# Weights' sign by a parametric ReLU, four q pairs shifted on VectorE, and the last attention product in 320 + 256 columns

## The chip, the cores and the metric

The kernel runs on one core of one Trainium2 chip. Its time is the device time of one launch in microseconds (us); lower is better. The kernel before took 1075.18 us, the median of 3 runs (1072.88 to 1076.26).

The engines are named as the profile names them. PE is TensorE, and PEld its weight loads. DVE is VectorE, ACT ScalarE (the engine of exp, ln and the other functions), POOL GpSimd. SP issues the transfers. Each engine runs its own instructions strictly in the order in which the program lists them; they wait for each other through semaphores.

## The reference

The work is a random-feature attention, and a two-layer network behind it:

```python
def phi(x):                                  # x is q or k, already scaled
    proj = np.einsum('bhsd,md->bhsm', x, omega)
    h = proj - np.sum(x * x, axis=-1, keepdims=True) / 2.0
    h = h - np.max(h, axis=-1, keepdims=True)
    return np.exp(h) / np.sqrt(m)
kv  = einsum('bhsm,bhsd->bhmd', phi(k), v);  z = sum_s phi(k)
out = einsum('bhsm,bhmd->bhsd', phi(q), kv) / (einsum('bhsm,bhm->bhs', phi(q), z) + 1e-6)
x = out.transpose(0, 2, 1, 3).reshape(4608, 512)
h = x @ w_in                                 # 512 -> 2048
g = h * erf(softplus(h))
return g @ w_out                             # 2048 -> 512
```

There are 8 batches, 8 heads, 576 tokens, 64 dimensions a head, and 128 random features. `w_in` and `w_out` arrive in float64; the kernel gets their bits as int64.

## The kernel before

**Attention.** Two heads make a pair, so there are 4 pairs a batch and 32 in all. A pair has 2 x 576 = 1152 token rows, in 9 chunks of 128. For k, and then for q, PE projects the chunks into three PSUM banks (`ppk`, `ppq`), DVE takes the negated maximum of each row (`mxk`, `mxq`), and ACT computes exp(projection + negated maximum), one instruction for each chunk, because the maximum is a bias with one value for each partition (`fk`, `fq`). PE multiplies `fk` with v (`kvp`), turns `fq` round by transposes (`pt`), and multiplies the two (`nd`), in spans of the 576 tokens: 384 columns, and then 192. ACT takes 1/denominator as exp(-ln(nd)) (`rc`), and DVE multiplies (`xs`). The first 8 pairs (batches 0 and 1) do this in plain float32; their squares (`uk`, `uq`) come from POOL or ACT and go into the projection. The other 24 pairs work with two-part numbers, a high part and a rest, in three matmuls each (`kh`/`kl`, `qh`/`ql`). There the squares are summed apart (`sk`, `sq`), and a pair of small DVE instructions (`shift`) puts them into the maxima.

**Network.** `h` (and `hX`, `hY`, `hZ` from the fourth batch on) is the first product, `o` the second; each is a sum of three matmuls of 288 columns, with weights in a high part and a rest. Between them stand softplus (`gs<-hs`), erf (`gs<-gs`), the gate, and the split of the result (`gh`, `gl`).

**Weights.** A unit of 128 x 512 weights comes as float64 bits (`st`) and is made into float32 in a PSUM tile (`wt`), 32 units in all, in the order in which the first batch needs them. Before the change a unit takes six steps: ACT scales the upper words by 2^-112 (`w_bias`, a Copy), DVE shifts left by 3 (`w_shift`), DVE puts the sign bit in (`w_sign`), DVE puts the last 3 bits in (`w_tail`), ACT rounds the high part (`w`), DVE takes the rest (`w`). A made unit is written back to DRAM (`wdw`) and fetched in later batches.

**The order.** `build` lists every operation with engines, costs and a due time, and `Plan.order` plays them through on a model of five engines, the ready operation with the earliest due time first. What comes out is the fixed order of each engine, and which of several engines takes a step (squares may go to POOL or ACT). `FIRST`, the time that a pair of the first batch is planned to take, sets the due times of the first batch, and by `START0` those of all that follow. The model charges ACT a change of function table only for operations that name a set (`set="exp"`, `"sp"`, `"erf"`), and holds other named sets back between the softplus and the erf of a chain (`lock`). The weights' steps name no set. Where the built program needs a table that isn't loaded, a load (ACT_TABLE_LOAD) is put in front of the instruction.

All compute instructions are recorded through one helper, so the profile gives them one line, L824; they are told apart by tile names. A name such as `uk_0_3` is batch 0, pair 3.

Of the kernel before, what the change touches and what calls it, by code (L numbers as in the profile page):

```python
# [19 lines left out]
P = 128  # L20
# [10 lines left out]
T = 288  # L31
# [273 lines left out]
SPANS = ((0, 384), (384, 192))  # L305

BLOCKS = ((("f", 0), ("f", 1)), (("e", 0),), (("f", 2),), (("e", 1),), (("f", 3),), (("e", 2),), (("e", 3),))
WHOLE = 8
PLAIN = 3
ROWS = 8  # L310
PAIR = 8.6
FIRST = 11.5
# [17 lines left out]
def build(emit):  # L330
# [46 lines left out]
    def make(u, t):  # L377
# [9 lines left out]
        pl.op("psign", [("V", 0.68, -1e9)], lambda e: E.w_sign(st, w), reads=[(st, 0), (w, 0)],  # L387
              writes=[(w, 0)])
# [109 lines left out]
    def project(n, qk, t0):  # L498
# [15 lines left out]
        else:  # L514
# [5 lines left out]
            order = range(3)  # L520
        for i in order:
            c = chunks[i]
            pl.op("max" + qk, [("V", 0.15 + 0.135 * len(c), -1e9)],
                  lambda e, i=i, c=c: E.maximum(mx, banks[i], c),
                  reads=[(banks[i], 0)], writes=[(mx, k) for k in c])
        if rows:
            sq = a["s" + qk]
            pl.op("less", [("V", 0.33, -1e9)], lambda e: E.shift(mx, sq),
                  reads=[(mx, k) for k in range(NC)] + [(sq, 0)], writes=[(mx, k) for k in range(NC)])
        for i in order:  # L530
            c = chunks[i]
# [275 lines left out]
def tile_attention_moe(ctx: ExitStack, tc: tile.TileContext, qT, kT, qR, kR, qN, kN, vP, omT, w1, w2, out):  # L807
# [68 lines left out]
    class Emit:  # L876
# [8 lines left out]
        def w_bias(self, e, t, w):  # L885
            dst, src = w.ap.bitcast(F32), t.ap[:, :, 1].bitcast(F32)
            if e == "A":
                act.activation(dst, src, AF.Copy, scale=2.0 ** -112)
            else:
                pool.tensor_scalar(dst, src, 2.0 ** -112, 0.0, op0=ALU.mult, op1=ALU.add)  # L890
# [275 lines left out]
```

## Time and profile before

| | before |
|---|---|
| median of 3 runs | 1075.18 us (1072.88 to 1076.26) |
| the profiled execution's own time | 1073.78 us |
| its span in the profile | 1072.0 us |
| granted TensorE clock, mean | 0.998 |
| PE busy | 1051.2 us, 8272 matmuls |
| DVE busy | 734.6 us |
| ACT busy | 719.4 us, 92 table loads among them |
| POOL busy | 352.1 us |

A row of the timeline gives start, length, engine, operation, out<-in, shapes and count, and in brackets the idle time before it with what ended that. A row of the windows gives a stretch, its length, and for each engine the busy time and instructions, then the granted clock, the share of time the DMA engines were busy, and GB/s. A row of the waits gives who waited for whom: the sum, how often, the longest. Matmuls are pipelined, so the distance from one start to the next tells what one costs, not its length.

### The profile page before, as it was taken

To read this page: it belongs to the slowest core of one execution; us is meant where nothing else is said; L and a number is where in the kernel's file an instruction comes from. 1 tells how busy PE (TensorE), PEld (TensorE's weight loads), DVE (VectorE), ACT (ScalarE), POOL (GpSimd) and SP (SyncE) were. 2 spreads that over 40 slices of the span, in tenths; PEclk is the share of its full clock that TensorE was granted. 3 is DMA by queue.
4 is the path that set the end of the run, shared out by engine and by line. 5 is a ranking of instruction groups with operands and counts; after the bars stand their busy time and mean duration, and the time that the engine had idled before them with its cause. 6 is when DMAs were issued, how large, how long until landed. Compare 5 with 4: busy or idle time off the path is not lost.

```text
span 1072.0 us, 21687 instructions
## 1 busy us (share of the span) xinstructions
PE 1051.2 (98%) x8272; PEld 1025.9 (96%) x8272; DVE 734.6 (69%) x1316; ACT 719.4 (67%) x1390; POOL 352.1 (33%) x306
## 2 busy tenths in 40 slices
PE   7899899999999999999999999999999999999998
PEld 7798899999999999999999999999999999999998
DVE  4889988877488586965768566766658656564431
ACT  7878878875668565867657666775667765564540
POOL 6222104100066294812334312522127222263330
PEclk9999999999999999999999999999999999999999
DMA  8376568776557777587776767768675775668771
GB/s 229 119 239 223 204 235 269 251 256 203 201 197 262 251 260 265 172 279 260 256 238 217 259 231 254 253 210 278 229 252 188 278 234 204 205 204 295 264 244 47
DMA packets 97382, 247.02 MB, mean 230 GB/s; under 512 B 10976, under 2 KB 11360, under 8 KB 97280
## 3 DMA queue, kind: packets, MB, share of 16 engines
q1 hardware_dynamic: 97216, 245.57, 67.9%
q8 instruction: 66, 1.08, 0.4%
q14 instruction: 36, 0.29, 0.1%
q0 software_dynamic: 64, 0.07, 0.0%
HBM read 210.99 MB, written 34.60 MB: 229 GB/s over the span
## 4 chain that ended last, share of the span: by engine, by line
PE 92%; DMA 3%; DVE 3%; ACT 1%; issue 1%; SPq 0%; POOL 0%; DVEq 0%; POOLq 0%; ACTq 0%
PE o L824 37%; PE h L824 13%; PE hX L824 12%; PE hY L824 6%; PE kvp L824 5%; PE nd L824 5%; PE ppq L824 4%; PE ppk L824 4%; PE hZ L824 3%; PE pt L824 2%; DMA st<-w 1%; DVE wt L824 1%; DMA uq<-qN 1%; DMA w<-wdw 1%; DVE xs L824 0%
## 5 line engine op out<-in xcount | busy, mean ns | idle before, releaser
L824 PE MATMUL o<-gh,w 128*128 128x288 f32 x2048 | 445.2, 298 | 0.2 <-ACT fq L824 0.2
L824 PEld LDWEIGHTS o<-gh,w 128*128 128x128 f32 x2048 | 339.3, 188 | 2.3 <-ACT fq L824 0.5
L824 PE MATMUL o<-gl,w 128*128 128x288 f32 x1024 | 301.7, 295 | 0.0
L824 PEld LDWEIGHTS o<-gl,w 128*128 128x128 f32 x1024 | 192.6, 188 | 0.0
L824 PE MATMUL h<-xh,w 128*128 128x288 f32 x768 | 174.6, 303 | 6.3 <-DVE w L824 2.8
L824 PE MATMUL hX<-xh,wb 128*128 128x288 f32 x640 | 162.0, 299 | 0.0
L824 PEld LDWEIGHTS h<-xh,w 128*128 128x128 f32 x768 | 129.7, 190 | 9.3 <-DVE w L824 4.5
L824 ACT ACT_TABLE_LOAD x92 | 118.0, 1283 | 2.3 <-PEq L1157 0.7
L824 PE MATMUL h<-xl,w 128*128 128x288 f32 x384 | 113.9, 297 | 0.0
L824 PEld LDWEIGHTS hX<-xh,wb 128*128 128x128 f32 x640 | 113.5, 188 | 0.4
L824 POOL TENSOR_TENSOR uk<-uk 128x288 f32<-128x288 f32 (+1 forms) x54 | 49.4, 934 | 181.4 <-DMA uk<-kN 119.9
L824 POOL TENSOR_TENSOR uq<-uq 128x288 f32<-128x288 f32 (+1 forms) x46 | 42.4, 942 | 184.5 <-DMA uq<-qN 66.1
L824 POOL TENSOR_TENSOR gl<-hs,gh 128x576 fp32r<-128x576 f32 x50 | 89.4, 1809 | 39.7 <-ACT gh L824 29.4
L824 PE MATMUL hX<-xl,wb 128*128 128x288 f32 x320 | 94.6, 296 | 0.0
L824 DVE TENSOR_REDUCE mxk<-ppk 128x4 f32<-128x512 f32 (+2 forms) x96 | 50.7, 553 | 62.1 <-PE ppk L824 61.1
L824 POOL TENSOR_TENSOR hs<-gs,hs 128x576 f32<-128x576 f32 x26 | 42.9, 1669 | 149.5 <-ACT gs L824 149.5
L824 DVE TENSOR_TENSOR hs<-gs,hs 128x1152 f32<-128x1152 f32 x51 | 81.2, 1600 | 13.4 <-ACT gs L824 13.4
L824 ACT ACTIVATE hs<-hX 128x288 f32<-128x288 f32 x75 | 30.8, 410 | 85.8 <-PE hX L824 82.9
L824 ACT ACTIVATE fq<-ppq,mxq 128x128 f32<-128x128 f32 x288 | 78.6, 386 | 13.5 <-DVE mxq L824 13.2
L824 ACT ACTIVATE rc<-nd,eps 64x192 f32<-64x192 f32 (+1 forms) x128 | 63.6, 497 | 33.3 <-PE nd L824 30.7
L824 ACT ACTIVATE fk<-ppk,mxk 128x128 f32<-128x128 f32 x288 | 79.9, 385 | 3.8 <-DVE mxk L824 3.3
L824 PE MATMUL hY<-xh,wb 128*128 128x288 f32 x320 | 81.3, 299 | 0.0
(106 smaller groups left out, 2115.9 us busy)
## 6 DMA issues: line engine op xcount, KB each, us to landing
w<-wdw SPq DMA_DIRECT2D x144, 512.0 KB, 4.9
wb<-wdcS SPq DMA_DIRECT2D x160, 256.0 KB, 4.1
wb<-wdw SPq DMA_DIRECT2D x120, 256.0 KB, 3.9
st<-w SPq DMA_DIRECT2D x32, 512.0 KB, 5.1
wdw<-w SPq DMA_DIRECT2D x32, 512.0 KB, 3.7
v<-vP SPq DMA_DIRECT2D x32, 325.0 KB, 4.3
out<-os SPq DMA_DIRECT2D x32, 288.0 KB, 3.6
wdcS<-cS SPq DMA_DIRECT2D x16, 512.0 KB, 5.1
```

What stands on the lines that cost most here:

```text
L824: return tc.keep_in_program_order(method(*args, **kwargs))
```

## The change

- **Sign.** `w_bias` becomes a parametric ReLU with scale 2^-112 and alpha -2^32. A negative word comes out positive, with its exponent 32 higher, and the shift by 3 moves that bit to the sign's place. `w_sign` goes, on all 32 units: three DVE steps instead of four.
- **q of the first four pairs.** For the pairs of batch 0, DVE adds the negated maximum to the projection, one instruction for each three chunks (`less`), and ACT takes one exponential over all nine chunks in place, instead of nine.
- **Raw maxima in PSUM.** In the 24 two-part pairs the maxima are written behind the middle chunk's bank in PSUM; the two small instructions read them there, the first writes back there, the second writes `mx`.
- **Spans.** `nd`, `rc` and `xs` work on 320 + 256 columns instead of 384 + 192, in all 32 pairs.
- **Planner.** `FIRST` goes from 11.5 to 10.0 (so `START0` from 51 to 45), and the cost of `nd` is written anew.

```diff
-SPANS = ((0, 384), (384, 192))
+SPANS = ((0, 320), (320, 256))
 WHOLE = 8
+LESS = [(n, "q") for n in range(NP)]
-FIRST = 11.5
+FIRST = 10.0
...
-        pl.op("psign", [("V", 0.68, -1e9)], lambda e: E.w_sign(st, w), reads=[(st, 0), (w, 0)],
-              writes=[(w, 0)])
...
+        less = (n, qk) in LESS
...
-                  lambda e, i=i, c=c: E.maximum(mx, banks[i], c),
-                  reads=[(banks[i], 0)], writes=[(mx, k) for k in c])
+                  lambda e, i=i, c=c: E.maximum(E.raw(banks[1]) if rows else mx.ap, banks[i], c),
+                  reads=[(banks[i], 0)], writes=[(banks[1], ("m", i))] if rows else [(mx, k) for k in c])
...
+            if less:
+                pl.op("less" + qk, [("V", 0.56, -1e9)], lambda e, i=i, c=c: E.less(f, mx, banks[i], c),
+                      reads=[(banks[i], 0)] + [(mx, k) for k in c], writes=[(f, k) for k in c])
+                continue
...
+        if less:
+            pl.op("exp" + qk, [("A", 1.16, -1e9)], lambda e: E.exponential_all(f),
+                  reads=[(f, k) for k in range(NC)], writes=[(f, k) for k in range(NC)], set="exp")
...
-                pl.op("nd", [("T", (4 if n < WHOLE else 3) * COST["mm"] * w / T, -1e9)],
+                pl.op("nd", [("T", w / 600 if n < WHOLE else 3 * max(0.111, 0.012 + w / 2400), -1e9)],
...
         def w_bias(self, e, t, w):
-                act.activation(dst, src, AF.Copy, scale=2.0 ** -112)
+            act.activation(w.ap.bitcast(F32), t.ap[:, :, 1].bitcast(F32), AF.Prelu, scale=2.0 ** -112,
+                           alpha=-2.0 ** 32)
...
-            for x in (-half_sq, half_sq):
-                dve.scalar_tensor_tensor(mx.ap, sq.ap, x, mx.ap, op0=ALU.mult, op1=ALU.add)
+            for dst, x in ((raw, -half_sq), (mx.ap, half_sq)):
+                dve.scalar_tensor_tensor(dst, sq.ap, x, raw, op0=ALU.mult, op1=ALU.add)
+
+        def less(self, f, mx, b, c):
+            n = len(c)
+            dve.tensor_add(f.ap[:, c[0]:c[0] + n, :], b.ap[:, :n * P].rearrange("p (c m) -> p c m", c=n),
+                           mx.ap[:, c[0]:c[0] + n].rearrange("p (c m) -> p c m", m=1).broadcast_to([P, n, P]))
+
+        def exponential_all(self, f):
+            act.activation(f.ap, f.ap, AF.Exp)
```

Since the planner decides the order, three places of the built program are shown. The first is DVE at q of batch 0, pair 1, and the first weight unit. Before:

```order
L824 TENSOR_REDUCE mxq_0_1_263<-ppq_0_1_0_253 128x3
L824 TENSOR_SCALAR wt1_0_0_257<-wt1_0_0_257 128x512
L824 TENSOR_REDUCE mxq_0_1_263<-ppq_0_1_1_259 128x3
L824 TENSOR_REDUCE mxq_0_1_263<-ppq_0_1_2_267 128x3
L824 SCALAR_TENSOR_TENSOR wt1_0_0_257<-st1_0_0_152,wt1_0_0_257 128x512 x2
L824 COPY kh_0_1_313<-kvp_0_1_287 128x2x64
```

And after:

```order
L832 TENSOR_REDUCE mxq_0_1_263<-ppq_0_1_0_250 128x3
L832 TENSOR_TENSOR fq_0_1_271<-ppq_0_1_0_250,mxq_0_1_263 128x384
L832 TENSOR_REDUCE mxq_0_1_263<-ppq_0_1_1_258 128x3
L832 TENSOR_REDUCE mxq_0_1_263<-ppq_0_1_2_267 128x3
L832 TENSOR_TENSOR fq_0_1_271<-ppq_0_1_1_258,mxq_0_1_263 128x384
L832 TENSOR_TENSOR fq_0_1_271<-ppq_0_1_2_267,mxq_0_1_263 128x384
L832 TENSOR_SCALAR wt1_0_0_254<-wt1_0_0_254 128x512
L832 COPY kh_0_1_302<-kvp_0_1_278 128x2x64
```

Three shifts came between the maxima, and of the unit's two steps on `st` (x2) one is left, which now stands further down.

The second place is ACT at the same pair, from the first unit's `wt` on. Before:

```order
L824 ACTIVATE wt1_0_0_257<-st1_0_0_152 128x512
L824 ACTIVATE rc_0_0_0_265<-nd_0_0_0_0_237,eps_68 64x384
L824 ACTIVATE rc_0_0_0_265<-nd_0_0_1_0_242,eps_68 64x384
L824 ACTIVATE fq_0_1_275<-ppq_0_1_0_253,mxq_0_1_263 128x128 x3
L824 ACTIVATE fq_0_1_275<-ppq_0_1_1_259,mxq_0_1_263 128x128 x3
L824 ACTIVATE fq_0_1_275<-ppq_0_1_2_267,mxq_0_1_263 128x128 x3
```

And after:

```order
L832 ACTIVATE wt1_0_0_254<-st1_0_0_154 128x512
L832 ACTIVATE rc_0_0_0_243<-rc_0_0_0_243 128x320
L832 ACTIVATE rc_0_0_1_265<-nd_0_0_0_1_245,eps_68 64x256
L832 ACTIVATE rc_0_0_1_265<-nd_0_0_1_1_247,eps_68 64x256
L832 ACTIVATE rc_0_0_1_265<-rc_0_0_1_265 128x256
L832 ACTIVATE uk_0_3_221<-uk_0_3_221 64x1152
L832 ACTIVATE wt1_0_1_292<-st1_0_1_160 128x512
L832 ACTIVATE fq_0_1_271<-fq_0_1_271 128x1152
```

The exponential of pair 1's q now stands behind the reciprocals of pair 0, the square of k of pair 3 (`uk_0_3`, POOL's work before) and a second unit's `wt`.

The third place is ACT at the second chain of softplus and erf (`gs` of the first batch, blocks 2 and 3). Before:

```order
L824 ACT_TABLE_LOAD
L824 ACTIVATE gs0_0_2_1190<-hs0_0_2_981 128x1152
L824 ACTIVATE w1_1_2_11_1030<-wt1_1_2_1109 128x2x256
L824 ACTIVATE w1_1_3_12_1053<-wt1_1_3_1118 128x2x256
L824 ACTIVATE gs0_0_3_1191<-hs0_0_3_1103 128x1152
L824 ACTIVATE wt2_0_0_0_1224<-st2_0_0_0_1194 128x512
L824 ACT_TABLE_LOAD
L824 ACTIVATE gs0_0_2_1190<-gs0_0_2_1190 128x1152
```

And after:

```order
L832 ACT_TABLE_LOAD
L832 ACTIVATE gs0_0_2_1097<-hs0_0_2_954 128x1152
L832 ACTIVATE w1_1_2_11_1000<-wt1_1_2_1054 128x2x256
L832 ACT_TABLE_LOAD
L832 ACTIVATE wt1_1_3_1141<-st1_1_3_1071 128x512
L832 ACTIVATE qh_1_1_1125<-pt_1_1_1_1137 128x384
L832 ACT_TABLE_LOAD
L832 ACTIVATE gs0_0_3_1098<-hs0_0_3_1047 128x1152
L832 ACT_TABLE_LOAD
L832 ACTIVATE wt2_0_0_0_1161<-st2_0_0_0_1100 128x512
L832 ACT_TABLE_LOAD
L832 ACTIVATE gs0_0_2_1097<-gs0_0_2_1097 128x1152
```

Each `wt` that falls between softplus and erf now has a table load of its own, and one brings softplus back where another softplus follows. The whole program has 102 table loads instead of 92: one more at the first chain, three more at each of the second, third and fifth.

More of the change, by code (lines that the diff above doesn't have):

```diff
@@ L523, in project @@
             pl.op("max" + qk, [("V", 0.15 + 0.135 * len(c), -1e9)],
-                  lambda e, i=i, c=c: E.maximum(mx, banks[i], c),
-                  reads=[(banks[i], 0)], writes=[(mx, k) for k in c])
+                  lambda e, i=i, c=c: E.maximum(E.raw(banks[1]) if rows else mx.ap, banks[i], c),
+                  reads=[(banks[i], 0)], writes=[(banks[1], ("m", i))] if rows else [(mx, k) for k in c])
         if rows:
             sq = a["s" + qk]
-            pl.op("less", [("V", 0.33, -1e9)], lambda e: E.shift(mx, sq),
-                  reads=[(mx, k) for k in range(NC)] + [(sq, 0)], writes=[(mx, k) for k in range(NC)])
+            keys = [(banks[1], ("m", i)) for i in order]
+            pl.op("less", [("V", 0.34, -1e9)], lambda e: E.shift(mx, E.raw(banks[1]), sq),
+                  reads=keys + [(sq, 0)], writes=keys[:1] + [(mx, k) for k in range(NC)])
         for i in order:
             c = chunks[i]
+            if less:
+                pl.op("less" + qk, [("V", 0.56, -1e9)], lambda e, i=i, c=c: E.less(f, mx, banks[i], c),
+                      reads=[(banks[i], 0)] + [(mx, k) for k in c], writes=[(f, k) for k in c])
+                continue
             pl.op("exp" + qk, [("A", 0.371 * len(c), -1e9)],
@@ L885, in w_bias @@
         def w_bias(self, e, t, w):
-            dst, src = w.ap.bitcast(F32), t.ap[:, :, 1].bitcast(F32)
-            if e == "A":
-                act.activation(dst, src, AF.Copy, scale=2.0 ** -112)
-            else:
-                pool.tensor_scalar(dst, src, 2.0 ** -112, 0.0, op0=ALU.mult, op1=ALU.add)
+            act.activation(w.ap.bitcast(F32), t.ap[:, :, 1].bitcast(F32), AF.Prelu, scale=2.0 ** -112,
+                           alpha=-2.0 ** 32)
         def w_shift(self, w):
             dve.tensor_scalar(w.ap, w.ap, 3, None, op0=ALU.logical_shift_left)
-        def w_sign(self, t, w):
-            dve.scalar_tensor_tensor(w.ap, t.ap[:, :, 1], -2 ** 31, w.ap,
-                                     op0=ALU.bitwise_and, op1=ALU.bitwise_or)
         def w_tail(self, t, w):
@@ L969, in project_mid, with raw, shift @@
             pe.matmul(b.ap[:, :P], lhsT=u.ap[:, NC * D + WIDE:], rhs=wr, start=True, stop=True)
+        def raw(self, mid):
+            return mid.ap[:, P:P + NC]
         def maximum(self, mx, b, c):
             n = len(c)
-            dve.tensor_reduce(mx.ap[:, c[0]:c[0] + n], b.ap[:, :n * P].rearrange("p (c m) -> p c m", c=n),
+            dve.tensor_reduce(mx[:, c[0]:c[0] + n], b.ap[:, :n * P].rearrange("p (c m) -> p c m", c=n),
                               axis=AX.X, op=ALU.max, negate=True)
-        def shift(self, mx, sq):
-            for x in (-half_sq, half_sq):
-                dve.scalar_tensor_tensor(mx.ap, sq.ap, x, mx.ap, op0=ALU.mult, op1=ALU.add)
+        def shift(self, mx, raw, sq):
+            for dst, x in ((raw, -half_sq), (mx.ap, half_sq)):
[6 more added lines that the diff above has]
+            act.activation(f.ap, f.ap, AF.Exp)
         def exponential(self, f, mx, b, c):
```

## The prediction

> **What bounds the kernel now.** I read the page's busy line first, then the windows, then who PE waited for.
>
> ```profile
> span 1072.0 us, 21687 instructions
> PE 1051.2 (98%) x8272; PEld 1025.9 (96%) x8272; DVE 734.6 (69%) x1316; ACT 719.4 (67%) x1390; POOL 352.1 (33%) x306
> ```
>
> PE is idle for 1072.0 - 1051.2 = 20.8 us in all. The windows say where:
>
> ```profile
> 0.00:52.00 52.00, 43.15 (x299) 38.06 (x300) 34.01 (x72) 42.16 (x120) 22.70 (x28) 1.00 0.65 179
> 52.00:100.00 48.00, 46.05 (x351) 44.45 (x349) 43.07 (x78) 39.12 (x82) 12.85 (x13) 1.00 0.67 225
> 100.00:150.00 50.00, 45.56 (x330) 42.38 (x330) 45.94 (x73) 40.48 (x79) 5.91 (x5) 0.97 0.56 194
> 150.00:200.00 50.00, 48.53 (x374) 46.52 (x374) 42.04 (x71) 40.63 (x84) 13.35 (x17) 1.00 0.78 271
> 200.00:1040.00 840.00, 839.72 (x6713) 826.60 (x6713) 562.97 (x1015) 555.47 (x1025) 293.15 (x242) 1.00 0.71 240
> 1040.00:1072.00 32.00, 28.15 (x213) 27.92 (x211) 6.57 (x10) 1.58 (x2) 4.13 (x3) 0.99 0.20 71
> ```
>
> From 200 to 1040 us PE idles for 0.3 us of 840: nothing done on DVE, ACT or POOL there can show, only PE's own work. The last 32 us lose 3.9 us, with hardly anything on ACT or DVE. What is left is the first 200 us: 8.9 us lost by 52 us (the first batch's attention), 2.0 + 4.4 from 52 to 150, 1.5 to 200. Whatever those 200 us gain or lose moves all that follows by as much, since what follows is PE alone. In 52 to 150 us DVE is the fuller helper, 43.07 + 45.94 = 89.0 of 98 us (91%), and ACT has 39.12 + 40.48 = 79.6 (81%).
>
> PE's waits up to 52 us:
>
> ```profile
> PE kvp L824 <- ACT fq L824: 1.3, 1, 1.3
> PE ppq L824 <- ACT fq L824: 0.9, 1, 0.9
> ```
>
> and from 52 to 210 us (sum, how often, longest):
>
> ```profile
> PE h L824 <- DVE w L824: 2.8, 3, 1.6
> PE h L824 <- ACT w L824: 1.6, 1, 1.6
> ```
>
> Early it is exponentials of q that hold a PSUM bank (1.3 + 0.9); later it is weight units not yet made (2.8 + 1.6).
>
> **The change part by part.** *Spans, in the 24 two-part pairs.* Starts of PE in one pair, columns in the shape:
>
> ```profile
> 227.03 0.29 PE L824 MATMUL h<-xl,w 128*128 128x288 f32 x1
> ...
> 227.29 0.34 PE L824 MATMUL nd<-qh,kh 128*128 128x384 f32 x1
> ...
> 227.81 0.25 PE L824 MATMUL nd<-qh,kh 128*128 128x192 f32 x1
> ...
> 228.46 0.32 PE L824 MATMUL h<-xh,w 128*128 128x288 f32 x1
> ```
>
> Two matmuls of 288 columns take 227.29 - 227.03 = 0.26, so 0.130 each; three of 384 take 0.52, so 0.173 each; six of 192 take 0.65, so 0.108 each. So 96 columns cost 0.043 above 288 and only 0.022 below it: 192 columns are too few to be worth their price. 320 lies a third of the way from 288 to 384, 0.144. 256 is 0.123 on the line from 192 to 288 and 0.116 on the line from 384 to 288 carried on. Against 0.173 + 0.108 = 0.281 the new pair of spans is 0.267 or 0.260, and there are 24 x 2 x 3 = 144 such couples: -2.1 or -3.1 us. If 256 cost as much as 288, -1.0. I take -2.5, and all of it counts, since it is PE's own work and most of it lies beyond 200 us. The eight float32 pairs have the same columns in all and a cost per column, so nothing there. ACT and DVE get the same 576 columns in two pieces as before.
>
> *Sign.* 64 DVE steps on `st` become 32:
>
> ```profile
> L824 DVE SCALAR_TENSOR_TENSOR wt<-st,wt x64: 681/695/730, 21.6 to 237.4; 128x512 int32<-128x512 int32 x64
> L824 ACT ACTIVATE wt<-st x32: 608/636/692, 19.3 to 233.8; 128x512 f32<-128x512 f32 x32
> ```
>
> That is 32 x 0.695 = 22.2 us off DVE, of which some 18 units, 12.5 us, lie between 52 and 150 us: DVE goes from 91% to 78% there. A parametric ReLU on ACT doesn't stand in this trace; the nearest row is the Copy it replaces (0.636), and the other functions of one immediate scale have the same rate by element, so I take 0.636, no change.
>
> *Table loads.* The order of the built program has ten more: one at the first chain of softplus and erf, three each at the second, third and fifth. The price of one, and what follows it:
>
> ```profile
> L824 ACT ACT_TABLE_LOAD x92 | 118.0, 1283 | 2.3 <-PEq L1157 0.7
> ...
> 96.39 0.88 ACT L824 ACTIVATE fk<-ppk,mxk 128x128 f32<-128x128 f32 x3
> 97.29 1.28 ACT L824 ACT_TABLE_LOAD   x1
> 98.58 1.16 ACT L824 ACTIVATE gs<-hs 128x1152 f32<-128x1152 f32 x1
> ```
>
> From the end of `fk` (97.27) to the start of softplus (98.58) is 1.31: a load costs its own 1.283. Seven of the ten fall before 150 us: 9.0 us, and ACT there goes from 79.6 to 88.6 of 98 us, 90%. So DVE and ACT change places. The three of the fifth chain lie beyond 200 us, where ACT is busy for 66% of the time, and are covered; uncovered they would be 3.8. The planner charges none of the ten. Behind the loads of the second chain stand the exponentials of k and q of batch 1's pair 2, and behind those, on PE, that pair's products. Bounds for 52 to 150 us: at best PE loses none of the weights' waits, -4.4, and with the clock that fell to 0.97 in 100 to 150 us (some 1.5 us of 50) -5.9; at worst the four loads of the first two chains come through to PE uncovered, 4 x 1.283 = +5.1 (the third chain's three then run while PE works off what it has). I take -1.0: ACT has 9.4 us left for the loads, so part of DVE's relief comes through.
>
> The Trainium skill, "ScalarE: Activation LUTs", section "What ACT_TABLE_LOAD costs", puts every change of set at about 1283 ns for the load and another 1380 ns of drain, some 2.66 us. By that the seven loads would be an estimated 18.6 us, more than ACT has left; the rows above show the 1283 and no drain behind it.
>
> *q of the first four pairs, and the start.* ACT's work for one q, the landing that matters, and the nearest row for the new steps of DVE:
>
> ```profile
> 17.81 0.93 ACT L824 ACTIVATE fk<-ppk,mxk 128x128 f32<-128x128 f32 x3
> 19.31 0.64 ACT L824 ACTIVATE wt<-st 128x512 f32<-128x512 f32 x1 [0.57 <-DMA st<-w]
> 19.98 1.18 ACT L824 ACTIVATE rc<-nd,eps 64x384 f32<-64x384 f32 x2
> 21.18 2.43 ACT L824 ACTIVATE fq<-ppq,mxq 128x128 f32<-128x128 f32 x9
> ...
> 25.93 2.25 POOL L824 TENSOR_TENSOR uk<-uk 64x576 f32<-64x576 f32 x2 [2.50 <-DMA uk<-kT]
> 26.24 1.07 PE L824 MATMUL pt<-ident,fq 128*128 128x128 f32 x6
> ...
> 52.45 0.43 PE L824 MATMUL h<-xh,w 128*128 128x288 f32 x1
> ...
> L824 DVE TENSOR_TENSOR ql<-pt,qh x72: 543/557/560, 188.7 to 920.5; 128x384 fp32r<-128x384 f32 x72
> ```
>
> One exponential over 1152 columns, 1.16 as the softplus above, for nine in 2.43: ACT saves 1.3 a pair, 5.1 in all. DVE pays three subtractions of 384 columns out of PSUM, 3 x 0.557 = 1.7 a pair, 6.7 in all, less 2.1 for the three signs that fall before 52 us: +4.6, on 34.0. The bank of `ppq` is freed by DVE now, so the 1.3 + 0.9 of PE's waits on `fq` should go.
>
> But ACT's order hides a new wait. The 25.93 row is the square of k of pair 3, which POOL could begin only when the tile had landed. The DMA engines are full until then:
>
> ```profile
> 20.00:26.00 6.00, 4.70 (x42) 4.50 (x41) 4.58 (x11) 5.83 (x17) 3.43 (x5) 1.00 1.03 290
> 26.00:30.00 4.00, 3.19 (x17) 1.76 (x16) 3.75 (x8) 3.56 (x12) 3.92 (x4) 1.00 0.26 96
> ```
>
> and SP's order puts the same bytes ahead of it as before (a weight unit moved up, but both units stood ahead already). So it lands at about 25.9 again, and the change puts this square on ACT, in front of `fq` of pair 1. ACT, done with `fk` at 18.74, has 3.6 us of `wt` and reciprocals (0.64 + 1.18, and about as much for the rest of pair 0) and reaches the square at 22.3; it stands until 25.9, then 1.16 (a square has the same 1152 columns), 0.64 and 1.16 bring `fq` of pair 1 at 28.9. Before, PE began that pair's transposes at 26.24. Queued behind are `fk` of pair 2 on ACT, and DVE's copies of `qh` behind PE's transposes. That is +2.7, with DVE's 4.6 closing some of the room to make it up, +1.0; less the 2.2 of waits that go: +1.5 by 52 us. Bounds: -2.2 (the square is made up for) and +3.7 (the waits on `fq` only change their name).
>
> *Raw maxima.* The two small instructions of each q and k of the 24 pairs are short, and begin late:
>
> ```profile
> L824 DVE SCALAR_TENSOR_TENSOR mxq<-sq,mxq x48: 170/171/1352, 167.7 to 907.9; 128x9 f32<-128x9 f32 x48
> ```
>
> Their number stays; only their operand moves. What 9 columns cost out of PSUM no row tells: not less than 0.170, and not more than the 0.557 above for 384 columns out of PSUM. Over 2 x 48 of them that is at most 96 x 0.387 = 37 us of DVE, which has 277 of 840 us free where most lie, and PE waits for no one there: 0 for the time, and nothing of the range. *FIRST* is only an order, and is in the places above.
>
> Sum: -2.5 - 1.0 + 1.5 = -2.0. The profiled execution took 1073.78 (span 1072.0 and 1.8 around it), so 1071.8; it stands 1.4 below the median, 1075.18, so for the median **1073.2 us**.
>
> **The rivals.** *Faster.* DVE's relief decides. For it: DVE is the fuller helper now, and three of PE's waits name its weights. Against: ACT takes on in the same stretch most of what DVE sheds. Waits on `fq` gone (-2.2), waits on weights gone (-4.4), spans -2.5: -9.1, 1066.
>
> *Slower.* ACT becomes the bound at the second chain. For it: seven loads in 98 us that the planner didn't count, in front of pair 2's exponentials, and an ACT already late from the start. Against: 9.4 us of ACT idle in that stretch. It decides as soon as ACT's busy share in 100 to 150 us goes above about 95%. Price: +2.7 from the start, +5.1 from four loads, -2.5: +5.3, 1080.5. One variant is that a load held ACT for longer than its own 1.28: with a drain as long again, four loads would cost 5.5 more, and the time would be 1086; the gap of 0.01 between load and softplus speaks against it, so 0.02 of the chance below. (That variant is the skill's rule named above.)
>
> *Near the forecast.* The two cancel, and PE's own 2.5 is what is left.
>
> **How the numbers follow.** About 0.3%, 3.2 us, is what a measurement of this kernel can tell from no change. Forecast 0.47, faster 0.33, slower 0.20. The forecast's own range is 1070 to 1077; of its chance 0.08 lies below 1072.0 and the rest is "same". Of the faster case 0.05 falls inside the 0.3%, of the slower 0.03, and 0.02 of the forecast's ends above. So faster 0.36, same 0.45, slower 0.19. All best bounds together give -3.1 - 5.9 - 2.2 = -11.2 (1064), all worst -1.0 + 5.1 + 3.7 = +7.8 (1083); the range, 1065 to 1079.5, leaves out about one in ten on each side.
>
> **What would show it.** Spans: starts of `nd` 0.144 and about 0.12 apart. Loads: 102 of 1.28 each, and ACT near 90% from 52 to 150 us. The start: ACT idle for 3 us or more before `uk`, named DMA, and the first `h` at 54 us or later instead of 52.45. The sign: no wait of PE for DVE's weights, and waits for ACT's `fk`, `fq` or `qh` in their place. Wrong would be: the first `h` before 51 us; PE losing less than 3 us between 52 and 150 (then 1066); more than 10 (then 1080); or any loss of several us beyond 200 us.

## The result: 0.6 to 0.8% slower

The changed kernel took 1084.06 us (median of 6 runs, 1079.27 to 1086.90), the kernel before 1075.09 in the same comparison: a ratio of 1.0083, with a 95% interval of 1.0056 to 1.0109. Timed twice more it took 1080.80 and 1081.02, ratios 1.0057 (1.0038 to 1.0075) and 1.0057 (1.0044 to 1.0071). The median of all 15 runs is 1081.37, and they spread over 7.6 us. Forecast were 1073.2, in a range of 1065 to 1079.5, and 1080.5 for the slower rival.

### The profile page after: what moved, and what is told of

It reads as the page before. It is cut to its first block, busy times and chain, and to the rows that moved or that the text cites. A ratio compares the mean times of both kernels' runs of the same rounds, so it can differ in the third digit from the quotient of the medians.

```text
span 1082.6 us, 21638 instructions
## 1 busy us (share of the span) xinstructions
PE 1052.5 (97%) x8272; PEld 1026.7 (95%) x8272; DVE 742.7 (69%) x1319; ACT 710.6 (66%) x1343; POOL 364.0 (34%) x319
## 4 chain that ended last, share of the span: by engine, by line
PE 87%; DVE 4%; ACT 4%; DMA 3%; issue 1%; POOL 1%; SPq 1%; DVEq 0%; ACTq 0%; POOLq 0%
PE o L832 35%; PE h L832 12%; PE hX L832 12%; PE hY L832 6%; PE kvp L832 5%; PE nd L832 4%; PE ppq L832 4%; PE ppk L832 3%; PE hZ L832 3%; PE pt L832 3%; ACT L832 1%; DMA uk<-kT 1%; ACT gs L832 1%; DVE wt L832 1%; DMA v<-vP 1%
## 5 line engine op out<-in xcount | busy, mean ns | idle before, releaser
L832 PE MATMUL h<-xh,w 128*128 128x288 f32 x768 | 177.0, 305 | 9.2 <-DVE hs L832 2.9
L832 ACT ACT_TABLE_LOAD x102 | 130.9, 1283 | 2.5 <-PEq L1169 0.7
L832 POOL TENSOR_TENSOR uk<-uk 128x288 f32<-128x288 f32 (+1 forms) x54 | 54.7, 1033 | 174.5 <-DMA uk<-kN 129.8
L832 ACT ACTIVATE rc<-nd,eps 64x256 f32<-64x256 f32 (+1 forms) x128 | 63.5, 496 | 44.8 <-PE nd L832 42.8
L832 DVE TENSOR_TENSOR hs<-gs,hs 128x1152 f32<-128x1152 f32 x50 | 74.5, 1501 | 15.7 <-ACT gs L832 15.5
L832 DVE TENSOR_REDUCE ppk<-ppk 128x4 f32<-128x512 f32 (+1 forms) x72 | 40.6, 564 | 55.7 <-PE ppk L832 54.6
L832 DVE TENSOR_TENSOR gl<-hs,gh 128x1152 fp32r<-128x1152 f32 x39 | 72.4, 1873 | 8.1 <-ACT gh L832 4.9
L832 PEld LDWEIGHTS h<-xl,w 128*128 128x128 f32 x384 | 73.4, 191 | 0.6 <-issue 0.2
```

Source lines behind the costliest of these rows:

```text
L832: return tc.keep_in_program_order(method(*args, **kwargs))
```

## The profile after

The page's busy line of the changed kernel, in an execution that took 1084.42 us:

```profile
span 1082.6 us, 21638 instructions
PE 1052.5 (97%) x8272; PEld 1026.7 (95%) x8272; DVE 742.7 (69%) x1319; ACT 710.6 (66%) x1343; POOL 364.0 (34%) x319
```

PE is idle for 1082.6 - 1052.5 = 30.1 us instead of 20.8, and busy for 1.3 us more. The stretches are those of before:

```profile
0.00:52.00 52.00, 41.90 (x274) 36.86 (x275) 34.17 (x75) 34.25 (x78) 15.39 (x20) 0.93 0.62 167
52.00:100.00 48.00, 46.39 (x355) 44.76 (x355) 35.89 (x66) 40.46 (x84) 13.83 (x15) 1.00 0.62 200
100.00:150.00 50.00, 42.86 (x295) 40.23 (x293) 40.61 (x68) 46.67 (x81) 6.12 (x8) 0.93 0.64 223
150.00:200.00 50.00, 48.79 (x385) 47.26 (x386) 42.12 (x72) 37.70 (x81) 10.50 (x13) 1.00 0.73 259
200.00:1040.00 840.00, 833.78 (x6678) 819.04 (x6677) 580.51 (x1028) 541.33 (x1013) 312.41 (x259) 1.00 0.71 237
```

Three rows carry the loss. Up to 52 us PE is idle for 10.1 us (before 8.9), and its granted clock has a mean of 0.93, where it was 1.00. From 100 to 150 us it is idle for 7.1 (before 4.4), with the clock at 0.93 instead of 0.97, and ACT has become the fullest engine: 46.67 of 50, where DVE had 45.94 before. And from 200 to 1040 us, where 0.3 us were idle before, 6.2 are.

**The start.** PE's longest wait up to 52 us, and ACT's rows there:

```profile
PE pt L832 <- ACT fq L832: 4.2, 1, 4.2
```

```profile
23.15 0.42 ACT L832 ACTIVATE rc<-rc 128x256 f32<-128x256 f32 x1
27.80 1.16 ACT L832 ACTIVATE uk<-uk 64x1152 f32<-64x1152 f32 x1 [4.23 <-DMA uk<-kT]
28.98 0.62 ACT L832 ACTIVATE wt<-st 128x512 f32<-128x512 f32 x1
29.54 1.15 ACT L832 ACTIVATE fq<-fq 128x1152 f32<-128x1152 f32 x1
```

This is the wait that the order showed: the square of pair 3's k (`uk`, at 27.80) stands on ACT until its tile has landed, and the exponential of pair 1's q (`fq`) behind it. PE waits for that 4.2 us. The first `h` starts at 57.6 us instead of 52.45.

**The second chain.** ACT from the second softplus to the exponentials of `fk`, and what PE waited for from 52 to 210 us:

```profile
99.24 1.28 ACT L832 ACT_TABLE_LOAD   x1
100.54 1.17 ACT L832 ACTIVATE gs<-hs 128x1152 f32<-128x1152 f32 x1
101.61 0.58 ACT L832 ACTIVATE w<-wt 128x512 fp32r<-128x512 f32 x1
102.20 1.28 ACT L832 ACT_TABLE_LOAD   x1
103.50 0.63 ACT L832 ACTIVATE wt<-st 128x512 f32<-128x512 f32 x1
104.06 0.47 ACT L832 ACTIVATE qh<-pt 128x384 f32<-128x384 f32 x1
104.55 1.28 ACT L832 ACT_TABLE_LOAD   x1
...
107.03 1.28 ACT L832 ACT_TABLE_LOAD   x1
108.32 0.62 ACT L832 ACTIVATE wt<-st 128x512 f32<-128x512 f32 x1
```

```profile
PE h L832 <- DVE hs L832: 2.9, 1, 2.9
PE h L832 <- ACT qh L832: 2.2, 1, 2.2
PE h L832 <- ACT hs L832: 1.4, 1, 1.4
```

The copy `qh` at 104.06 frees the PSUM bank that PE's next `h` needs, and stands behind a load of 1.28 us and a unit (`wt` at 103.50) that is in no hurry. The 2.9 come by way of DVE:

```profile
108.98 0.70 DVE L832 TENSOR_SCALAR wt<-wt 128x512 int32<-128x512 int32 x1 [3.06 <-ACT wt L832]
110.99 0.45 DVE L832 COPY hs<-h 128x288 f32<-128x288 f32 x1
```

DVE waits 3.06 us for ACT's `wt` at 108.32, which stands behind two loads, and only behind that unit's steps makes the copy `hs` that frees PE's next bank. PE's waits for the weights themselves (2.8 + 1.6 before) have shrunk to 0.2.

**The clock.** PE's window rows in steps of 3.41 us, first at the start, then at the second chain (PE's busy time is the second number, the granted clock the third from the end):

```profile
26.46:29.87 3.41, 0.11 (x1) 0.00 (x0) 0.93 (x2) 2.05 (x3) 1.75 (x2) 0.99 0.52 172
29.87:33.29 3.42, 2.55 (x10) 2.00 (x11) 1.39 (x3) 2.91 (x9) 1.30 (x2) 0.50 0.00 1
33.29:36.70 3.41, 3.41 (x8) 2.30 (x8) 2.93 (x6) 3.00 (x8) 0.00 (x0) 0.51 0.27 107
...
101.47:104.88 3.41, 0.84 (x5) 0.60 (x6) 3.34 (x6) 3.36 (x6) 0.00 (x0) 1.00 0.67 226
104.88:108.29 3.41, 3.41 (x14) 3.01 (x13) 1.04 (x2) 3.38 (x3) 2.25 (x2) 0.50 0.96 320
108.29:111.71 3.42, 0.49 (x3) 0.25 (x3) 2.68 (x5) 3.38 (x5) 0.00 (x0) 1.00 0.36 144
111.71:115.12 3.41, 3.41 (x16) 3.41 (x16) 3.41 (x4) 3.38 (x6) 0.00 (x0) 0.50 0.27 105
```

After a step at full clock in which PE was busy for less than about half, the next one runs at half clock. Four steps run at half clock here, two at the start and two at the second chain, and one in the kernel before (at 102 us). Each halves the work of up to 3.41 us, so three more cost at most 3 x 1.7 = 5.1 us; they cost less where PE would have stood waiting in that time anyway (e1, e5 and e9 below). This is also why PE's busy time rose although its work fell.

**Beyond 200 us.** The two longest waits of PE there, and the rows of ACT, DVE and PE at the first of them:

```profile
PE h L832 <- issue: 2.4, 1, 2.4
PE hX L832 <- ACT hs L832: 1.3, 1, 1.3
```

```profile
212.56 1.28 ACT L832 ACT_TABLE_LOAD   x1
213.86 0.62 ACT L832 ACTIVATE wt<-st 128x512 f32<-128x512 f32 x1
214.41 0.42 ACT L832 ACTIVATE kh<-kvp 128x128 fp32r<-128x128 f32 x2
215.12 0.48 DVE L832 TENSOR_TENSOR kl<-kvp,kh 128x128 fp32r<-128x128 f32 x2
215.70 0.37 PE L832 MATMUL h<-xh,w 128*128 128x288 f32 x1 [2.39 <-issue]
```

The profile names no releaser for the 2.4, but the built program does: this `h` lies in the PSUM bank that `kvp` had, and waits for `kl`, the last reader of `kvp`. `kl` ends at 215.60, 0.1 us before `h` starts. It needs `kh`, and `kh` stands on ACT behind two more loads and a unit: `kvp` was ready at 210.08, and `kh` starts at 214.41. In e2 below, without the loads, the same `kh` starts 0.1 us after its `kvp`, and PE does not wait there. This is in the fifth chain, whose three loads were to be covered.

## The experiments

All ratios are to the kernel before on the same chip in the same comparison (medians of 1075.09 to 1075.60 us). Not all experiments ran on one chip, and differences between them below are of medians. The edits are shown shortened. "Mixed" is the kernel of e10.

| kernel | median us | ratio, 95% interval |
|---|---|---|
| changed kernel (three times) | 1084.06, 1080.80, 1081.02 | 1.0083, 1.0057, 1.0057 |
| e1 before + spans | 1077.26 | 1.0012 (0.9999 to 1.0024) |
| e2 changed, loads out (and no sign) | 1072.55 | 0.9972 (0.9960 to 0.9985) |
| e3 changed, square on POOL | 1078.42 | 1.0026 (1.0017 to 1.0036) |
| e4 both e2 and e3 | 1068.47 | 0.9934 (0.9919 to 0.9949) |
| e5 parametric ReLU held back, square on POOL | 1078.60 | 1.0029 (1.0015 to 1.0043) |
| e7 changed, sign on DVE | 1081.31 | 1.0054 (1.0039 to 1.0069) |
| e8 before + parametric ReLU | 1076.97 | 1.0016 (1.0005 to 1.0026) |
| e9 changed, PE kept busy | 1082.20 | 1.0058 (1.0037 to 1.0079) |
| e10 mixed; again (e16) | 1070.86; 1070.28 | 0.9953 (0.9937 to 0.9970); 0.9950 (0.9937 to 0.9962) |
| e11 mixed, maxima in SBUF | 1070.90 | 0.9954 (0.9938 to 0.9970) |
| e12 mixed, q as before | 1072.44 | 0.9972 (0.9957 to 0.9987) |
| e13 mixed, all signs on DVE | 1077.74 | 1.0014 (0.9999 to 1.0029) |
| e14 mixed, 384 + 192; again (e17) | 1068.57; 1070.24 | 0.9934 (0.9912 to 0.9957); 0.9944 (0.9932 to 0.9956) |
| e15 mixed, FIRST 11.5 | 1078.95 | 1.0024 (1.0011 to 1.0037) |

### The loads and the square, each taken away in an order that stays

**e2.** The table loads go, and nothing moves. The kernel then leaves out the sign of the weights:

```diff
-act.activation(w, t[:, :, 1], AF.Prelu, scale=2.0 ** -112, alpha=-2.0 ** 32)
+act.activation(w, t[:, :, 1], AF.Copy, scale=2.0 ** -112)
```

> The changed kernel with Copy in place of the parametric ReLU. The order of every engine is that of the changed kernel; only the table loads between softplus and erf are gone, 11 of them. The sign of the weights is left out of the computation. Theory (the loads of the second chain stop PE and the clock falls after that): PE's idle time from 100 to 122 us falls from about 7 to under 3 us, the clock dips there shrink (they cost some 3.4 us), the 2.4 us wait at 215 us goes: 1075 to 1077.5. Rival (loads lie beside other work; the order itself is at fault): at most 2 us gained, 1082 or more.

**e3.** One instruction goes to another engine, after the planner has made the order:

```diff
 for o in plan.order(slots, CAPS):
+    if o.name == "sqk" and any(t.name == "uk_0_3" for t in o.uses):
+        o.eng = "G"
```

> The changed kernel with one instruction moved: the square of k of pair 3 (uk) goes from ACT to POOL, as in the kernel before; all else keeps its order. Theory (this square on ACT costs the start 4.2 us of wait and 3.3 us of clock): the first exponential of pair 1's q starts about 25 us instead of 29.5, PE's wait for it falls below 1 us, no clock dip from 30 to 37 us, first h some 5 us earlier, time 1076 to 1079. Rival (DVE, fuller by 4.6 us in the start, takes the wait over): first h at most 2 us earlier, 1081 to 1083.

**e4.** Both edits.

> Both edits at once: Copy in place of the parametric ReLU (no sign, 11 loads fewer) and the square of pair 3's k on POOL. Theory (two separate causes): the gains add, 1067.5 to 1071.5, below the kernel before by the spans and a little of DVE's relief. Rival (the gain of one is taken up by a wait of the other or by the new order): 1074 or more.

Measured: 1072.55, 1078.42, 1068.47: e2 gains more than its theory gave it, e3 and e4 lie inside theirs. The gains add to within the spread, so these are two separate causes. **The loads cost 1078.42 - 1068.47 = 10.0 us.** Eleven loads are 14.1 us of ACT; so 70% of them came through to the end. **The square costs 1072.55 - 1068.47 = 4.1 us** where the loads are out, and 2.4 to 5.6 where they are in (against 1080.80 and 1084.06). ACT and PE from 87 to 110 us, which holds the second chain, of e3 and then of e4:

```profile
87.00:110.00 23.00, 15.85 (x102) 14.97 (x101) 19.55 (x27) 22.83 (x35) 2.25 (x2) 0.85 0.61 216
```

```profile
87.00:110.00 23.00, 19.00 (x127) 17.25 (x126) 22.35 (x32) 21.59 (x39) 2.25 (x2) 0.96 0.61 219
```

With the loads ACT is busy for 22.83 of 23 us, and PE stands for 7.2 us of them at a clock of 0.85. Without them PE stands for 4.0 at 0.96. The first `o` starts at 128.3 us in e3 and at 123.0 in e4: of the 8.8 us between these two executions, 5.2 are lost by then. The first `hX` starts at 443.1 and 434.1: 3.8 more are lost between, 2.4 of them PE's wait at the fifth chain, which is gone in e2 and e4.

**e6 and e18.** The changed kernel, twice more.

> The changed kernel once more, on the chip of its neighbours here. Theory (its own landing of pair 3's k varies between launches and the square waits for it on ACT; with the square on POOL the time was 1078.42, and the square cost 1072.55 - 1068.47 = 4.1 without the loads): about 1082.5, runs spread over 5 us or more. Rival (the first comparison was of a chip of its own): within 1 us of 1078.4.

> The changed kernel once more, as the common base of the sums. Theory (its time hangs on when the tile of pair 3's k lands, anew in each launch): median between 1080 and 1084.5, runs spread over 4 us or more. Rival (a chip of its own made the first 1084): 1080 to 1081, spread under 2 us.

Measured: 1080.80 (1080.01 to 1084.31), between theory and rival, and 1081.02 (1079.71 to 1083.78), as the theory has it. Of the three executions with a profile, two have the square at 27.80 and 27.45 and took 1084.42 and 1084.31. In the third, of e18, the tile landed early, and it took 1079.71:

```profile
23.75 1.16 ACT L832 ACTIVATE uk<-uk 64x1152 f32<-64x1152 f32 x1 [2.11 <-DMA uk<-kT]
25.50 1.15 ACT L832 ACTIVATE fq<-fq 128x1152 f32<-128x1152 f32 x1
```

About 4 us of landing go with 4.6 to 4.7 us at the end, in these three. Order and transfers are the same, and the transfer was issued at 15.32, 15.65 and 14.84, so most of the difference arose after the issue. Such a wait at the head of a busy engine can make a kernel's time spread: with the square on POOL (e3) ten runs spread over 2.2 us, the 15 of the changed kernel over 7.6. It is not the only source, for e12, which has the square on POOL too, spreads over 5.7.

### The spans alone

**e1.** The kernel before with one line changed:

```diff
-SPANS = ((0, 384), (384, 192))
+SPANS = ((0, 320), (320, 256))
```

> The kernel before with the spans 320 + 256 and nothing else of the change. Theory (spans are worth what the starts of PE said): matmuls of 320 columns start 0.144 us apart and those of 256 about 0.12, PE's work without clock losses falls by 2.5 to 3.5 us, and the time is 1071.5 to 1073. Rival (another split moves PE's order and opens new waits beyond 200 us, as the 5.9 us there in the changed kernel could mean): PE's work falls as much, but its idle time from 200 to 1040 us rises from 0.3 to 2 us or more, and the time is 1074 to 1077.

Measured: 1077.26, no faster, at most 0.24% slower. PE's idle time from 200 to 1040 us rose only from 0.3 to 1.0, so the rival's place is wrong too. In the execution with a profile the loss seems to be here:

```profile
98.35:101.76 3.41, 1.60 (x5) 0.90 (x6) 3.41 (x6) 3.40 (x4) 2.02 (x2) 0.96 0.83 291
101.76:105.17 3.41, 2.45 (x10) 2.10 (x9) 3.34 (x5) 3.39 (x4) 1.92 (x1) 0.50 0.86 293
105.17:108.59 3.42, 2.35 (x5) 1.73 (x6) 3.35 (x5) 3.41 (x12) 0.00 (x0) 0.50 0.04 14
```

The planner made another order of it; PE falls below half of a step at the second chain, and then stays at half clock for five steps, 17 us, in the first of which it is busy for 2.45 us. But the half clock is not shown to be what costs the time: over the ten executions the time does not follow the granted clock. The fastest (1075.24) had a mean of 0.992, the slowest (1078.79) one of 0.996. In that stretch PE also waits for other engines, 2.0 us for `fk` and 1.3 for DVE's weights. Where the gain of the spans went in this kernel stays open.

### Ways to have the sign without the loads

**e5.** The planner is told what table the parametric ReLU needs, so that it holds it back between softplus and erf; the square is on POOL:

```diff
 pl.op("pbias", [("A", 0.67, -1e9)], lambda e: E.w_bias(e, st, w),
-      reads=[(st, 0)], writes=[(w, 0)])
+      reads=[(st, 0)], writes=[(w, 0)], set="exp")
```

> The changed kernel with the weights' parametric ReLU named as needing the table of the exponentials, so that the planner charges it and holds it back between softplus and erf (92 table loads instead of 102), and with the square of pair 3's k on POOL. Complete and with the sign. Theory (the loads were what made the parametric ReLU dear, and units that come a chain later are early enough): like the kernel without the sign, which took 1068.47 us: 1067 to 1071. Rival (units held back for a chain come too late, and PE waits for weights instead): 1073 to 1077.

Measured: 1078.60, 7.6 us above the theory, and above the rival's 1077 too. There are 92 loads, but PE now waits for the weights that were held back:

```profile
PE h L832 <- ACT w L832: 4.4, 1, 4.4
```

From 97.0 to 114.1 us its clock is at half for five steps, as in e1; and here too the execution with the profile, at a mean clock of 0.991, was the fastest of eight (1077.23; the slowest, 1080.30, had 0.990). In this order a unit that comes a chain later is too late.

**e7.** The sign part undone, the rest of the change as it is (the square too stays on ACT), planned anew.

```diff
-act.activation(w, t[:, :, 1], AF.Prelu, scale=2.0 ** -112, alpha=-2.0 ** 32)
+act.activation(w, t[:, :, 1], AF.Copy, scale=2.0 ** -112)
...
+pl.op("psign", [("V", 0.68, -1e9)], lambda e: E.w_sign(st, w), reads=[(st, 0), (w, 0)], writes=[(w, 0)])
```

> The changed kernel with the sign part undone: Copy and the fourth DVE step again, no extra table loads, all else as in the change, planned anew. DVE has 22.2 us more, some 17 of them before 150 us. Theory (the loads were the harm, and DVE's relief is worth some us of itself): 1073 to 1077, above the 1072.55 of the kernel that has neither sign nor loads. Rival (DVE's relief is worth nothing): 1072 to 1073.

Measured: 1081.31, above both. No load is added, and PE waits for DVE's weights (`PE h <- DVE w`, 5.5 us, and two of `o`, 1.3), with four half-clock steps, two of them in the start, and a first `h` at 56.3. So DVE's relief was worth much more than the prediction gave it, but the new order does not let it be priced here. What e7 does show: with the whole sign part undone, relief and loads both, the change is as slow as with it (e6, on the same chip, 1080.80).

**e8.** The kernel before with the sign part alone: 99 loads instead of 92.

```diff
-act.activation(dst, src, AF.Copy, scale=2.0 ** -112)
+act.activation(w, t[:, :, 1], AF.Prelu, scale=2.0 ** -112, alpha=-2.0 ** 32)
...
-pl.op("psign", ...)
```

> The kernel before with the parametric ReLU and without the sign step, and nothing else of the change: 99 table loads instead of 92. Theory (each load before 150 us comes through to PE, since DVE and PE both wait for ACT there): six loads of 1.28 are 7.7 us, less 2 to 4 us of waits for weights that DVE's relief ends: 1078 to 1082. Rival (in the order of the kernel before ACT has room for the loads): 1071 to 1074.

Measured: 1076.97, 0.16% slower, between theory and rival. In this order the loads and the relief nearly cancel.

**e10.** The order of the changed kernel, square on POOL. Where a unit's step falls between softplus and erf, it is the old Copy, and DVE's sign step follows; everywhere else it is the parametric ReLU. Seven units go the old way:

```diff
+if table[0] == "sp":          # the set that ACT holds at this place of the order
+    between.add(w)
+    act.activation(w, t[:, :, 1], AF.Copy, scale=2.0 ** -112)
+    return
 act.activation(w, t[:, :, 1], AF.Prelu, scale=2.0 ** -112, alpha=-2.0 ** 32)
...
+if w in between:
+    dve.scalar_tensor_tensor(w, t[:, :, 1], -2 ** 31, w, op0=ALU.bitwise_and, op1=ALU.bitwise_or)
```

> The order of the changed kernel, with the sign: the parametric ReLU where the loaded table has it, and the old Copy with the DVE sign step behind it for the 7 units that fall between softplus and erf; the square of pair 3's k on POOL. 91 table loads. Theory (what the kernel without the sign gained was the loads' going, and 7 DVE steps of 0.7 us add little): 1068 to 1071. Rival (DVE is on the path there as ACT was, 3 of the 7 steps lie at the second chain): 1072 to 1075.

Measured: 1070.86, and 1070.28 when timed again (e16, below), as the theory has it. It beats both kernels, by 0.5% (before) and 1.0% (after). Against e4, which has no sign step at all, its seven cost about 2 us.

**e13.** The same order with all 32 units the old way.

```diff
-if table[0] == "sp":
+if True:
```

> As the mixed kernel, in the same order, but all 32 units with Copy and the sign step on DVE: 25 more DVE steps of 0.7 us, no table load more or less. This prices DVE's relief alone. Theory (relief and loads are worth about as much: 7 sign steps cost some 2 us between the kernel without sign and the mixed one, and some 10 more of these steps lie before 150 us): 1074 to 1079. Rival (DVE has room; the relief was worth the 1 us that the prediction gave it): 1071 to 1072.

Measured: 1077.74, inside the theory. The 25 steps are 25 x 0.695 = 17.4 us of DVE, and **6.9 us of them reach the end** (6.6 by the ratios): DVE's relief is worth that in this order. With the seven steps of e10, all 32 come to about 9 us, against 10.0 for the loads: e3, with all of the loads and none of the steps, is 0.7 us slower than e13, which has it the other way round. So the sign part as a whole is worth nothing clear of noise, here as in e7, and costs 0.16% in e8. The row of 100 to 150 us shows DVE at the limit, as the kernel before had it:

```profile
100.00:150.00 50.00, 45.41 (x337) 43.59 (x337) 47.80 (x80) 39.56 (x81) 6.12 (x8) 0.97 0.61 212
```

### The clock

**e9.** The changed kernel, with transposes that nobody reads ahead of the three long waits:

```diff
+WARM = (("pt_0_1_0", "pt_0_1_0", 32), ("h000_1_1", "pt_1_1_2", 18), ("h010_1_0", "nd_1_1_0_0", 24))
+for key, bank, n in WARM:
+    if o.eng == "T" and key in [t.name for t in o.alloc]:
+        for _ in range(n):
+            pe.transpose(out=names[bank].ap[:, 384:512], in_=ident, identity=ident)
```

> The changed kernel with useless transposes of the identity on PE, into PSUM columns that nobody reads, at the three places where PE stands longest: 32 ahead of the transposes of pair 1 (4.2 us), 18 and 24 ahead of the two waits of h at 102 and 108 us (2.2 and 2.9 us). No wait is shortened and nothing else moves. Theory (half the harm is the clock: a stretch of 3.41 us in which PE works less than half is followed by one at half clock): the dips at 30 to 37 and at 103 to 115 us go, which cost some 5 us; 1075 to 1078 against 1080.8 and 1084.06. Rival (the clock falls for another reason, or PE would have waited anyway in the time that the half clock took): 1080 to 1084.

Measured: 1082.20, no gain, as the rival has it. The dips at the start are gone and one of those at the second chain is left (another came at 211 us), so the clock does follow from PE's idle time. But in the execution that was profiled the tile landed at 25.04, and the 32 transposes, which last until 29.17, held PE back by themselves; and at the second chain `h` still waited for DVE's `hs` (1.9 us), which waits for ACT. How much of the loss is the clock's is not settled by this, but filling the waits, which left two of four half-clock steps, gained nothing.

### The other parts

**e11.** Mixed, with the maxima in SBUF:

```diff
-lambda e, i=i, c=c: E.maximum(E.raw(banks[1]) if rows else mx.ap, banks[i], c)
+lambda e, i=i, c=c: E.maximum(mx.ap, banks[i], c)
```

> As the mixed kernel, with the raw maxima back in SBUF and the two small DVE instructions as they were. Theory (raw maxima are worth nothing, and the 4 us that PE idles beyond 200 us in all kernels with the new order are the planner's): within 1.5 us of the mixed kernel, PE's idle time from 200 to 1040 us again 3 to 5 us. Rival (the small instructions that wait on PSUM hold DVE, and these waits beyond 200 us are theirs): that idle time under 1.5 us, and the time 2.5 to 4 us lower.

Measured: 1070.90 against 1070.86, and 3.3 us of idle time beyond 200 us, as the theory has it. Raw maxima are worth nothing at the end.

**e12.** Mixed, with `LESS = []`, planned anew.

> As the mixed kernel, with q of the first four pairs as before (nine exponentials from PSUM, no subtraction on DVE), planned anew. Theory (ACT's 1.3 us and DVE's 1.7 us a pair about cancel): first h 50 to 52 us, within 2 us of the mixed kernel. Rival (ACT sets the pace of the start, 5.1 us are worth having): first h at 53 us or later, 2.5 to 5 us slower than the mixed kernel.

Measured: 1072.44 and a first `h` at 51.8 instead of 50.3: about 1.5 us, inside the theory; the two intervals overlap.

**e15.** Mixed, with `FIRST = 11.5`, planned anew.

> As the mixed kernel, with FIRST back at 11.5. Theory (the planned pace of the first batch shifts due times alone): 1069 to 1073. Rival (the tighter pace is what opens the waits beyond 200 us): PE idle from 200 to 1040 us under 2 us instead of 4.5, 1067 to 1069.

Measured: 1078.95, which neither foresaw. PE waits 3.5 us for a copy `qh` of ACT in the first batch, and the first `h` starts at 55.7. A planner's number that costs no instruction moved the time by 8 us, by way of the order.

**e14, and e16 and e17 on one chip.** Mixed with the spans 384 + 192, planned anew, and mixed as it is.

> As the mixed kernel, with the spans 384 + 192 and planned anew with them. Theory (spans are worth PE's 3.5 us where no new wait eats them): PE's busy time 3 to 4 us higher, 1073.5 to 1075. Rival (which waits the planner's order opens weighs more than the 3.5): the time moves by less than 1.5 us or by more than 6.

> The mixed kernel once more, beside the next one on one chip. Theory (the new spans save PE 1.5 us of work and open 4 us of waits beyond 200 us): 1069.5 to 1071.5. Rival (the 2.3 us between 1070.86 and 1068.57 were the chips' difference): within 1 us of its neighbour.

> The mixed kernel with the spans 384 + 192 once more. Theory (spans as before are the better ones here): 1068 to 1069.5, 1.5 to 3 us below its neighbour. Rival: within 1 us of its neighbour.

Measured: 1068.57 in e14, which neither of its guesses had, and side by side 1070.28 with the new spans (e16) and 1070.24 with the old (e17): no difference, as the rivals of both have it. What the new spans save is spent again beyond 200 us, e16 first, then e17:

```profile
200.00:1040.00 840.00, 835.47 (x6681) 821.02 (x6680) 578.48 (x1018) 537.22 (x1003) 316.88 (x260) 1.00 0.72 239
```

```profile
200.00:1040.00 840.00, 839.85 (x6701) 826.37 (x6701) 541.79 (x989) 555.14 (x1037) 308.45 (x252) 1.00 0.71 239
```

PE is idle for 4.5 us there with the new spans, and for 0.15 with the old. With the new spans DVE is busy for 36.7 us more there, with 29 instructions more, and ACT has 34 fewer: the planner gives DVE copies that ACT has with the old. So the 3.8 us of idle time that the changed kernel has there beside the wait at the fifth chain belong to the order that comes with the spans in this kernel; in e1, with the same spans in the kernel before, it was 1.0.

## Why the prediction was wrong

The direction was wrong: "The two cancel, and PE's own 2.5 is what is left" was likeliest, and the slower rival, to which the prediction gave 0.20, is what happened. In the order of the changed kernel, held still, the sum can be set beside the runs (us, differences of medians):

| term | forecast | measured |
|---|---|---|
| all else: spans, start without the square, new order (e13 against before) | -2.5, and 1.5 - 2.7 = -1.2 | +2.3 |
| sign part: loads against DVE's relief (e3 against e13) | -1.0 | +0.7 |
| square of pair 3's k on ACT (changed against e3) | +2.7 | +2.4 to 5.6 |
| sum | -2.0 | +5.4 to 8.6 |

The largest miss is the first row, 6.0 us (e13 carries its sign steps in an order that was not planned for them). **The step that failed is "nothing done on DVE, ACT or POOL there can show", said of 200 to 1040 us, with "all of it counts" for the spans that rests on it.** PE waits 6.2 us there where it waited 0.3, and the spans are worth nothing (e16, e17). What e12 prices of the start, 1.5 us for q, has the sign and about the size of the forecast; what else the new order costs in that row stays open. Step by step:

- **Table loads: mis-sized.** Their count and price are as worked out (102, 1283 ns each), and nothing behind them either: `gs` starts 0.02 after a load's end, so the drain that the Trainium skill's page "ScalarE: Activation LUTs", section "What ACT_TABLE_LOAD costs", adds does not show here. (The variant's 5.5 us for a drain "as long again" would be 4 x 1.283 = 5.1; no drain showed.) But the worst bound said that four loads come through, +5.1, "the third chain's three then run while PE works off what it has" and the fifth's "are covered". e3 against e4: 10.0 us, 3.8 of them after the first `o`. The room of 9.4 us in 98 that the prediction counted on isn't at the chains: ACT is busy for 22.83 of 23 us around the second, and in the changed kernel for 3.36 to 3.38 of each 3.41 from 101 to 115 us.
- **DVE's relief: mis-sized as well.** The bound for it was PE's visible waits for weights, 4.4 us. e13 prices it at 6.9 for 25 of the 32 steps, and all 32 come to about 9. Loads and relief were both about twice their bound, so that their balance came out within 2 us of the -1.0 is luck.
- **The start: right in kind.** The wait of ACT for pair 3's tile was foreseen (exponential of pair 1 at 28.9, measured 29.54; first `h` at 54 or later, measured 57.6). Its price, +2.7, is 2.4 to 5.6. The landing was taken to be as before, 25.9; it differs between executions, 23.75 to 27.80, and with the early one the first `h` starts at 51.8. The 2.2 us of waits on `fq` did go.
- **The clock: left out.** A dip of 1.5 us stood in the profile of before, and the prediction counted only that it could go. Waits that a new order makes bring new half-clock steps: four instead of one. What they cost is not priced: filling the waits (e9) gained nothing.
- **Spans: work sized right, gain not.** The starts:

```profile
302.19 0.31 PE L832 MATMUL nd<-qh,kh 128*128 128x320 f32 x1
...
302.63 0.28 PE L832 MATMUL nd<-qh,kh 128*128 128x256 f32 x1
...
237.80 0.28 PE L832 MATMUL nd<-qh,kh 128*128 128x256 f32 x1
...
238.51 0.29 PE L832 MATMUL h<-xh,w 128*128 128x288 f32 x1
```

  0.44 / 3 = 0.147 for 320 columns and 0.71 / 6 = 0.118 for 256, together 0.265 instead of 0.281: -2.3 us over 144, forecast -2.5. But "all of it counts, since it is PE's own work" was false: the spans give the planner other operations, and in its new order PE waits for 4.5 us where it waits for 0.15 with the old spans (e16 and e17).
- **Beyond 200 us.** "any loss of several us beyond 200 us" was named as what would make the prediction wrong, and 6.2 us are lost there: 2.4 by the fifth chain's loads, the rest with the spans' order.
- **Parametric ReLU, q, raw maxima.** `wt` on ACT takes 636 ns as the Copy did, the subtraction 548 ns (taken 557), the exponential over 1152 columns 1156 (taken 1160). Raw maxima: 166 to 172 ns each, and nothing at the end (e11).

The slower rival had the right places in the first 150 us, and 5.3 us where 5.4 to 9.0 were measured. That its number comes so near is partly luck: it has loads of 5.1 for 10.0, no relief for about 9, and 2.5 from the spans that did not come. Its chance was weighed by ACT's mean share, which was to go above about 95% from 100 to 150 us; it went to 93%, and the loads came through all the same.

## What to carry to other kernels

Where a function moves to another engine, look at what table that engine holds at each place it will stand, and use the new form only where it is free: with the square on POOL and the order held, 25 of 32 units made the kernel 0.5% faster than before (e10), all 32 made it 0.3% slower (e3), and none left it level with before within the noise (e13). A mean busy share of 80 to 90% hides the place where an engine's queue is on the path; look at the row of the chain itself. And with a planner that orders everything, an edit is never alone: FIRST alone moved the time by 8 us, so parts are priced in an order that is held still, as in e2 to e4 and e13. A clear price of one half, such as the 10.0 us of the loads, is not yet the price of the part: the other half has to be priced in the same order. One way was not tried: behind an erf the parametric ReLU needed no load (`wt` at 96.14 of the changed kernel, behind the erf at 94.79), but ahead of one it got a load of its own, and the erf another (107.03 and 108.97), so a load of erf's table ahead of such a unit might serve both.

## What the runs showed of the hardware

- **The granted clock goes in steps of 3.41 us on a fixed grid.** In the first 157 us of all profiles here, after their first 6 us, a step at full clock in which PE was busy for 1.66 us or less was followed by one at half clock (27 times; one with 1.62 was not), and one with 1.76 or more was not. So the bound lies near one half. At half clock, 3.41 us busy brought the full clock back, 2.87 or less did not, and about 3.1 went either way (e7 and e10). 2.87 us at half clock are 1.4 us of work at the full clock, so the same bound may hold for work; that is not shown. The Trainium skill, "TensorE: Matmul & The Clock Gate", section "What's actually happening", gives a free-running window of 3413 ns, and the traces agree. Idle gaps shorter than the window were enough here (2.22 and 2.93 us at the second chain).
- **Half clock can last, and a lower clock need not be a slower run.** In e1 and e5 PE stayed at half clock for 17 us, while the engines it waits for kept it short of the bound. Yet the fastest of eight executions of e5 (1077.23 us) had a mean clock of 0.991, where four at 0.995 took 1078.03 to 1078.70, and the fastest of ten in e1 (1075.24) had 0.992, the slowest 0.996. In e18 the slowest did have the lowest clock (1083.78 at 0.990, against 1079.71 at 0.997). Where PE waits for others, its half clock need not add to the time.
- **The landing of a transfer varied by 4 us between executions** of the same kernel (its reader started at 23.75, 27.45 and 27.80 us; it was issued at 14.84, 15.65 and 15.32), while the DMA engines were full (mean busy share 0.95 to 1.10 in every 2 us from 18 us until it landed). Why it varied is not shown.
